# Mamba2 scan with a low-rank mixer on one Trainium2 core: the first batch's transposes split over two banks, the second weight's conversions put elsewhere, and the later loads paced

## The chip, the cores and the metric

The kernel runs on one core of one Trainium2 chip. The metric is the device time in microseconds (us) of one execution; the figure for the kernel before is the median of 7 runs. One execution was also profiled: every instruction of TensorE (PE, with its weight loads as PEld), VectorE (DVE), ScalarE (ACT), GpSimd (POOL) and of SyncE's DMA queue (SP) has a start and a duration there.

## The reference

The first half is a chunked state-space scan over x (4 batches, 8 heads, 768 steps, 32 channels) with B and C (16 states) and a decay a. The second half mixes the tokens through a low rank, then applies a two-layer network to the channels.

```python
# for each batch, head and chunk of the sequence
CB = C_chunk @ B_chunk.T                          # scores
y_intra = (CB * L) @ x_chunk                      # L = exp(cum_i - cum_j), causal
y_inter = (C_chunk @ state) * exp(cum)
state = decay_full * state + sum_j(B_j x_j exp(cum_last - cum_j))
# then, with x = y of all heads, (4, 768, 256)
h = x.T @ U @ V                                   # U 768x32, V 32x768
u = x + h.T
out = u + relu(u @ w_ch1) @ w_ch2                 # w_ch1 256x1024, w_ch2 1024x256
```

x, a, B and C are float32. U, V and the two weights arrive as float64, so the kernel loads their 64-bit words and makes float32 of them itself.

## The kernel before, in words

**Tiling.** A batch's 768 steps are three pairs of 128-step blocks; the twelve pairs of the four batches are numbered k = 0 to 11 (pairs 0 to 2 are batch 0). For a pair, `prep` (L339, DVE) multiplies B and C by decay factors into `BC`. `decayed` (L351, POOL) makes `bd`. `turning` (L363) transposes the four 128x128 pieces of `BC` on PE, and ACT copies them out as `T` (both B and C) and as `Cm` (C, twice, each time masked to one of the two heads of a 32-row group). `gram` (L398) multiplies B by `Cm` into four PSUM banks, and `mask` (L410, DVE) applies causality to give `M`. `state` (L429, PE) and `update` (L444, DVE, then POOL for `Sm`) carry the state on. `inter` (L499) and `intra` (L528) add both parts of y in two `y` banks, and `yout` (L542, ACT) copies them to `yT`. `inter` comes in two parts, and the first product of part 1 is made to wait for some instruction that comes after part 0: the entry `behind["part"]`, which `apart` (L469) sets to a one-column copy that waits for part 0.

**The mixer** of a batch: `ytokening` (L551) transposes `yT` back to `ytok`; `project` (L579) multiplies by U into `pT`; `mixed` (L592) multiplies by V and adds into `yT`. `spread` (L884) puts V on all partition groups first. For batch 0, `up` (L696) then makes `gT` = relu(u @ w1) in 16 steps (m = 0 to 7, two halves each; `some(2)` runs one m), and `whole` (L806) and `down` (L708) multiply by w2. Batches 1 to 3 use a form with fewer products (`quad`, L623; `down`'s p1 to p7), which needs sums of weight blocks (`operands`, L1010) and sums of gT blocks (`sums`, L716).

**Weights.** `to_fp32` (L299) converts one load in three steps: (1) DVE `e` and `top`, ACT `rest`; (2) ACT `power`; (3) three DVE instructions. The loads in order are U with V, two eighths of w1, three quarters of w1, and four quarters of w2. `convert(n)` (L865) issues the next n steps. `convert_ahead` (L869) issues steps 1 and 2 of the next load but one and then step 3 of the current one. Of w2's four quarters, before, steps 3 come at m = 3, m = 5, before m = 6 and before m = 7.

**Order.** The order on every engine is written out by hand: L906 to L996 for batch 0, then the loop at L1028, where iteration k runs pieces of the mixer, the transposes of pair k + 2, `inter(k, 0)`, `gram(k + 1)`, `intra(k)`, `state(k + 1)`, `mask(k + 1)`, `inter(k, 1)`, `yout(k)` and `update(k + 1)`. Iterations 3 and 4 hold the last pieces of batch 0's `up`; iteration 5 begins with the two `whole`. [...]

**Loads.** All loads stand on SP's queue in program order, ahead of all stores of the output (`store`, L757). A pair has six: B and C of each block (64 KB each) and x of each block (128 KB each). Pairs 4 to 11 follow the weights. A pair's buffers are one of six.

**PSUM.** There are eight banks, two under each of the tags w, x, z and y, taken in turn. `gram` uses `xxzz`. `fill(n)` makes the next bank begin with an idle product of n x 128 columns, whose result is overwritten (L82).

```python
        if engine:                                # L386, in turning
            nc.scalar.copy(out=s["T"][:, :, c:c + n], in_=tp)
    turn(0, 1, 1, "w", nc.vector)                 # L913: Cm by DVE, then T by ACT, one bank
    for pieces in plan[:2]:                       # L996: iterations 3 and 4 begin with
        pieces.insert(0, convert_ahead)           # steps of w2's conversion
        if k + 2 < last:                          # L1052
            prep(k + 2)
            decayed(k + 2)
```

Of the kernel before, what the change touches and what calls it, by code (L numbers as in the profile page):

```python
# [9 lines left out]
FP32 = mybir.dt.float32  # L10
# [5 lines left out]
ALU = mybir.AluOpType  # L16
# [4 lines left out]
def kernel(  # L21
# [64 lines left out]
    def bank(tag, *dims):  # L86
        t = psum.tile([P, *dims], FP32, tag=tag, name=tag, bufs=BANKS[tag])
        if fills[0]:
            idle(t if len(dims) == 1 else t.rearrange(
                {2: "p a b -> p (a b)", 3: "p a b c -> p (a b c)"}[len(dims)]), fills[0])  # L90
        fills[0] = 0
        return t

    def fill(n):


        fills[0] = n
# [7 lines left out]
        in_=a.rearrange("(g b) h (c s) -> g (b h c) s", g=2, s=P).rearrange(  # L105
            "g r s -> r g s"))

    x_sb, bc_sb = {}, {}
    pairs = [(b, q) for b in range(NB) for q in range(NPR)]

    def load_bc(k, blocks=(0, 1)):
        b, q = pairs[k]
        if k not in bc_sb:
            bc_sb[k] = raw.tile([P, 2, 2, NH, N], FP32, tag="bc", name="bc")
        for c in blocks:
            for i, src in enumerate((B, C)):
                nc.sync.dma_start(
                    out=bc_sb[k][:, i, c],
                    in_=src[b, :, ts(2 * q + c, P), :].rearrange("h s n -> s h n"))

    def load_x(k, blocks=(0, 1)):
        b, q = pairs[k]
        if k not in x_sb:
            x_sb[k] = raw.tile([P, 2, NH, D], FP32, tag="x", name="x")
        for c in blocks:
            nc.sync.dma_start(
                out=x_sb[k][:, c],
                in_=x[b, :, ts(2 * q + c, P), :].rearrange("h s d -> s h d"))


    UV = const.tile([P, 2, NC * RK], FP32)
# [49 lines left out]
    for m in range(0, NM, 2):  # L181
        load_words(w2[:, m:m + 2],
                   w22[m * P:(m + 2) * P].rearrange("(m p) d -> p m d", p=P))
    for k in range(NPR + 1, NB * NPR):
        load_bc(k)
        load_x(k)


    ident = const.tile([P, P], FP32)
# [170 lines left out]
                :, :, None].to_broadcast([P, n * NH, N]),  # L360
            op=ALU.mult)

    def turning(k, c=0, n=2, tag="w", engine=None):  # L363

        s = st[k]
        if c == 0:
            s["T"] = att.tile([P, 2, 2, P], FP32, tag="T", name="T", bufs=3)
            s["Cm"] = att.tile([P, 2, 2, P], FP32, tag="Cm", name="Cm", bufs=3)
        tp = bank(tag, 2, n, P)
        for i in range(2):  # L370
            for v in range(n):
                if i or v:
                    yield
                nc.tensor.transpose(out=tp[:, i, v],  # L374
                                    in_=s["BC"][:, i, c + v].rearrange("p h n -> p (h n)"),
                                    identity=ident)
        if not engine:
            nc.scalar.copy(out=s["T"][:, :, c:c + n], in_=tp)
        for i in range(2):
            if engine:  # L380
                engine.tensor_scalar(out=s["Cm"][:, i, c:c + n], in0=tp[:, 1],
                                     scalar1=slot[:, i, None], scalar2=None, op0=ALU.mult)
            else:
                nc.scalar.activation(s["Cm"][:, i, c:c + n], tp[:, 1], AF.Copy,  # L384
                                     scale=slot[:, i, None])
        if engine:  # L386
            nc.scalar.copy(out=s["T"][:, :, c:c + n], in_=tp)
# [10 lines left out]
    def gram(k):  # L398
        s = st[k]
        s["g"] = g = four("xxzz", 2, 2, H)  # L400
        for c in range(2):
            for p in range(2):
                for r in range(4):
                    rows, cols = ts(r, Q), ts(p, H)
                    nc.tensor.matmul(  # L405
                        out=g[r][cols, c], lhsT=s["T"][rows, 0, c, cols],
                        rhs=s["Cm"][rows, :, c, cols], start=(c == 0), stop=True,
                        skip_group_check=True)
# [165 lines left out]
    def mixer(b):  # L574
# [4 lines left out]
        def project(c0=0, c1=NC):  # L579

            if c0 == 0:
                hold["p"] = bank("w", P)
            p = hold["p"]
            for c in range(c0, c1):
                for q in range(4):
                    nc.tensor.matmul(out=p[ts(q, Q)], lhsT=U_sb[:, c],  # L586
                                     rhs=ytok[b][:, c, ts(q // 2, P)],
                                     start=(c == 0), stop=(c == NC - 1), skip_group_check=True)
            if c1 == NC:
                nc.scalar.copy(out=pT, in_=p)  # L590

        def mixed():  # L592

# [289 lines left out]

    def spread():  # L884

        v = [bank("y", HS // 2) for _ in range(2)]
        for q in range(4):
            for i in range(2):
                rows = ts(2 * (q % 2) + i, Q)
                nc.tensor.matmul(out=v[i][ts(q, Q)], lhsT=ident[rows, rows], rhs=Vq[rows],  # L890
                                 start=True, stop=True, skip_group_check=True)
        for i in range(2):
            nc.scalar.copy(out=V4[:, ts(i, HS // 2)], in_=v[i])

    def hold(load, until):

        tc.add_manual_dep(load.ins, until.ins.name, mybir.DependencyInfo(
            mybir.DependencyClass.Sync, mybir.DependencyReason.DATA))

    one, others = slice(0, 1), slice(1, NB)  # L900
    yT[0] = mix.tile([P, NCB, S], FP32, tag="yT", name="yT")
# [8 lines left out]
    prep(0, 1, 1)  # L910
    decayed(0)
    fill(1)
    turn(0, 1, 1, "w", nc.vector)  # L913
    fill(2)
    gram(0)
    prep(1, 0, 1)
# [20 lines left out]
    prep(2, 1, 1)  # L937
    decayed(2, 1, 1)
    update(1)
    turn(2, 1, 1, "x", nc.vector)  # L940
    intra(1)
    fill(1)
    gram(2)
    state(2)
    hold(held[0], mask(2, (0, 1)))
    update(2)
    hold(held[2], mask(2, (2, 3)))
    inter(1, 0)
    apart(nc.scalar.copy)
    inter(1, 1)  # L950
    yout(1)
    convert(2)
    fill(1)
    ytokens(0, "x")
    intra(2)
    inter(2, 0)
    apart(nc.vector.tensor_copy)
    inter(2, 1)
    yout(2)
    ytokens(1)  # L960
    convert(1)
    fill(1)
    ytokens(2, "z", (nc.vector.tensor_copy,) * 2)
    spread()
    convert(3)
    next(steps.pop(0))
    project()
    mixed()
    convert(2)
    convert(2)  # L970
# [7 lines left out]
    keep(others)  # L978
    prep(3)
    decayed(3)  # L980
    convert_ahead()
    some(2)
    convert_ahead()
    some(2)
    turn(3)
    prep(4)
    decayed(4)
    some(2)
    gram(3)
    state(3)  # L990
    mask(3)
    update(3)
    convert_ahead()
    some(2)
    turn(4)
    for pieces in plan[:2]:  # L996
        pieces.insert(0, convert_ahead)


    ws = const.tile([P, 5, DF // 2], FP32)  # L1000
# [27 lines left out]
    for k in range(NPR, last + 1):  # L1028
        b, q = divmod(k, NPR)
        pieces = plan[q] if q or b == 1 else []  # L1030
        turns = [turning(k + 2).__next__] * 4 if k + 2 < last else [lambda: None]
        if k > NPR:
            tokens = [ytokening(k - 1).__next__] * 3
            if q == 0:
                late = downs
                project, mixed, ups, plan, downs = mixer(b - 1)
                p4 = late.pop()
                pieces = (late[:1] + tokens + late[1:7] + [project] + late[7:11] + [mixed]
                          + late[11:])
# [12 lines left out]
        if k + 2 < last:  # L1052
            prep(k + 2)
            decayed(k + 2)
        run(pieces + turns)
        inter(k, 0)
        if k + 1 < last:
            gram(k + 1)
        else:
            settle()  # L1060
        intra(k)
        if k + 1 < last:
            state(k + 1)
            mask(k + 1)
        inter(k, 1)
        yout(k)
        if k + 1 < last:
            update(k + 1)
        if q == 1:
            run(plan[3])  # L1070
        if k == NPR + 1:
            operands(4, nc.vector)
    run(downs)

# [29 lines left out]
```

## Time and profile before

| | us |
|---|---|
| median of 7 runs | 239.86 |
| lowest and highest run | 238.24, 243.35 |
| the profiled execution, its own time | 240.84 |
| its span, first to last instruction | 239.0 |

| engine | busy us | share of the span | instructions |
|---|---|---|---|
| PE | 228.4 | 96% | 3166 |
| PEld | 175.6 | 73% | 3166 |
| DVE | 155.1 | 65% | 363 |
| ACT | 95.6 | 40% | 245 |
| POOL | 20.6 | 9% | 40 |

The 16 DMA engines moved 14.60 MB in 81909 packets, of which 76052 were under 512 bytes. The row of granted TensorE clock shows 9 tenths or more in all slices.

A row of the timeline is: start, time taken, engine, line, instruction, what is written from what, shapes, how many alike; then in square brackets how long the engine stood idle just before, and what ended the wait. "issue" means that the engine waited for nothing that the profile shows. Durations of neighbours overlap by about 0.1 us, since the next instruction starts before the last one is recorded as ended. The table of windows gives the busy time of each engine in a stretch, with the number of instructions in brackets.

### The profile page before, as it was taken

The numbers are of one execution on the slowest core, as the hardware profiler recorded it, in microseconds if no ns is written. First come the engines' busy times: TensorE is split into PE (matmuls) and PEld (weight loads), VectorE is DVE, ScalarE is ACT, GpSimd is POOL, SyncE is SP. The second block draws the span as 40 slices with busy tenths as digits, with TensorE's granted clock in tenths as the row PEclk, the third lists the DMA queues.
The fourth block names the chain that finished last, engine by engine and source line by source line (L and its number), as shares of the span: only waits on it lengthen the run. The fifth ranks groups of instructions, "written<-read, shape, count | busy, mean of one in ns | idle before, by whom it ended". The sixth has DMA issues, their size and how long they took to land.

```text
span 239.0 us, 7374 instructions
## 1 busy us (share of the span) xinstructions
PE 228.4 (96%) x3166; PEld 175.6 (73%) x3166; DVE 155.1 (65%) x363; ACT 95.6 (40%) x245; POOL 20.6 (9%) x40
## 2 busy tenths in 40 slices
PE   7998899897899999999999999999999999999995
PEld 5666556555688988565799987565799896659994
DVE  3675799797996667475896671556974372478511
ACT  5354558755514312537624112456312014663110
POOL 4221001120330300002021100010000000000000
PEclk9999999999999999999999999999999999999999
DMA  6984959998988810100001010000001011000111
GB/s 80 115 112 137 274 66 313 157 113 95 115 106 105 130 46 0 44 3 3 3 3 47 5 44 17 31 3 0 3 3 47 8 38 44 0 0 3 44 47 45
DMA packets 81909, 14.60 MB, mean 61 GB/s; under 512 B 76052, under 2 KB 80084, under 8 KB 81876
## 3 DMA queue, kind: packets, MB, share of 16 engines
q1 hardware_dynamic: 81876, 14.13, 32.4%
q8 instruction: 25, 0.41, 0.7%
q14 instruction: 8, 0.07, 0.1%
HBM read 10.98 MB, written 3.15 MB: 59 GB/s over the span
## 4 chain that ended last, share of the span: by engine, by line
PE 83%; DVE 10%; ACT 3%; issue 3%; POOL 0%; DVEq 0%; POOLq 0%; ACTq 0%
PE x L741 17%; PE x L633 14%; PE z L741 13%; PE z L633 10%; PE y L537 4%; PE y L515 3%; PE x L405 3%; PE x L816 3%; PE w L557 2%; PE w L586 2%; PE w L438 2%; PE x L82 2%; PE w L374 1%; DVE rest L323 1%; PE x L737 1%
## 5 line engine op out<-in xcount | busy, mean ns | idle before, releaser
L633 PE MATMUL x<-t,ws 128*128 128x384 f32 x72 | 28.7, 496 | 0.0
L741 PE MATMUL x<-w2s,words 128*128 128x128 f32 x176 | 23.2, 275 | 0.0
L741 PEld LDWEIGHTS x<-w2s,words 128*128 128x128 f32 x176 | 21.6, 193 | 0.0
L621 ACT ACTIVATE gT<-gT 128x384 f32<-128x384 f32 x36 | 19.0, 528 | 2.4 <-DVE gT L642 2.3
L465 POOL TENSOR_TENSOR Sm<-S,slot 128x256 f32<-128x256 f32 (+1 forms) x12 | 8.8, 736 | 122.3 <-DVE S L458 91.8
L633 PEld LDWEIGHTS x<-t,ws 128*128 128x128 f32 x72 | 12.5, 190 | 8.0 <-ACT top L638 1.3
L730 DVE TENSOR_TENSOR words<-gT 128x512 f32<-128x512 f32 (+1 forms) x28 | 16.7, 598 | 0.6 <-ACT gT L621 0.6
L642 DVE TENSOR_TENSOR gT<-z,top 128x384 f32<-128x384 f32 x12 | 6.7, 558 | 15.2 <-PE z L633 13.4
L417 DVE TENSOR_TENSOR M<-x,causal 128x256 int32<-128x256 int32 x24 | 9.1, 420 | 9.6 <-PE z L405 8.3
L638 ACT COPY e<-x 128x384 f32<-128x384 f32 x12 | 5.8, 479 | 23.1 <-PE x L633 23.1
L549 ACT COPY yT<-y 128x256 f32<-128x256 f32 x24 | 7.8, 375 | 17.3 <-PE y L515 17.3
L799 ACT COPY o<-x 128x128 f32<-128x128 f32 x11 | 2.9, 266 | 28.6 <-PE x L741 28.6
L458 DVE SCALAR_TENSOR_TENSOR S<-S,kept,w 128x64 f32<-128x64 f32 x40 | 11.2, 280 | 3.5 <-PE w L438 1.8
L405 PE MATMUL x<-Cm,T 32*64 32x128 f32 x192 | 12.0, 291 | 1.1 <-ACT Cm L384 0.7
L701 PE MATMUL x<-yT,w 128*128 128x384 f32 x32 | 12.0, 496 | 0.7 <-DVE yT L601 0.6
L741 PE MATMUL x<-w,gT 128*128 128x128 f32 x88 | 12.6, 285 | 0.0
L676 DVE TENSOR_SCALAR gT<-x 128x384 f32<-128x384 f32 x12 | 6.7, 557 | 9.1 <-PE x L633 9.1
L741 PEld LDWEIGHTS x<-w,gT 128*128 128x128 f32 x88 | 10.8, 191 | 2.3 <-issue 1.6
L741 PE MATMUL z<-w2s,words 128*128 128x128 f32 x88 | 11.9, 278 | 0.0
L356 POOL TENSOR_TENSOR bd<-bc,FD 128x256 f32<-128x256 f32 (+1 forms) x13 | 9.4, 721 | 29.5 <-ACT FD L282 20.0
L537 PE MATMUL y<-M,x 64*32 64x64 f32 x768 | 10.7, 224 | 1.1 <-issue 1.1
L515 PE MATMUL y<-T,Sm 32*64 32x64 f32 x352 | 11.0, 230 | 0.7 <-ACT settled L471 0.4
(179 smaller groups left out, 507.3 us busy)
## 6 DMA issues: line engine op xcount, KB each, us to landing
words<-in_moe_w_ch_dram SPq DMA_DIRECT2D x7, 512.0 KB, 6.0
x<-in_x_dram SPq DMA_DIRECT2D x24, 128.0 KB, 3.4
out_dram<-o SPq DMA_DIRECT2D x11, 256.0 KB, 2.1
bc<-in_B_dram SPq DMA_DIRECT2D x24, 64.0 KB, 3.6
bc<-in_C_dram SPq DMA_DIRECT2D x24, 64.0 KB, 3.0
words<-in_moe_w_ch_dram SPq DMA_DIRECT2D x2, 256.0 KB, 3.5
words<-in_moe_V_dram SPq DMA_DIRECT2D x1, 192.0 KB
words<-in_moe_U_dram SPq DMA_DIRECT2D x1, 192.0 KB, 4.9
```

The source lines that it names most:

```text
L356: nc.gpsimd.tensor_tensor(out=st[k]["bd"][:, c:c + n].rearrange("p c h n -> p (c h) n"), in0=bc_sb[k][:, 0, c:c + n].rearrange("p c h n -> ...
L405: nc.tensor.matmul(out=g[r][cols, c], lhsT=s["T"][rows, 0, c, cols], rhs=s["Cm"][rows, :, c, cols], start=(c == 0), stop=True, skip_group_ ...
L417: done = nc.vector.tensor_tensor(out=M[:, r].bitcast(INT32).rearrange("p c s i -> p (c s) i"), in0=g[r].bitcast(INT32).rearrange("p c s i ...
L458: done = nc.vector.scalar_tensor_tensor(out=new, in0=st["S", b], scalar=kept[:, b, j, None], in1=add, op0=ALU.mult, op1=ALU.add)
L465: nc.gpsimd.tensor_tensor(out=s["Sm"][:, sl], in0=s["S"][:, sl].rearrange("p i (s d) -> p i s d", s=2), in1=slot[:, None, :, None].to_broa ...
L515: product = nc.tensor.matmul(out=y[p][ts(r % 2, H), r // 2, c], lhsT=own[ts(r, Q)], rhs=s["T"][ts(r, Q), 1, c, ts(p, H)], start=fresh(k, p ...
L537: nc.tensor.matmul(out=y[p][ts(i, Q), n, c], lhsT=x_sb[k][half, c, h], rhs=s["M"][half, h // 2, c, h % 2], start=fresh(k, p, [i]), stop=Tr ...
L621: nc.scalar.activation(g, g, AF.Relu)
L633: nc.tensor.matmul(out=X[name], lhsT=lhsT[:, ts(i, P)], rhs=rhs, start=start, stop=True, skip_group_check=True)
L701: nc.tensor.matmul(out=g, lhsT=w1[:, n, ts(m, P)], rhs=uT[:, n, ts(k, HS)], start=(n == 0), stop=(n == NCB - 1))
L730: nc.vector.tensor_tensor(out=S[v][:, lo:hi], in0=l[:, lo:hi], in1=r[:, lo:hi], op=op)
L741: nc.tensor.matmul(out=X[name], lhsT=lhsT[:, i], rhs=rhs[:, i], start=start and u is None and i == 0, stop=True, skip_group_check=True)
```

## The change

1. The helper `hold` moves up. Each of the six loads of pairs 7 to 11 waits until the load two before it has landed. Loads up to pair 6 are as before.
2. `turn(0, 1, ...)` and `turn(2, 1, ...)` become `split`: C is transposed first and into a bank of its own (y or z), B into another (w or x). ACT copies B's half of `T` alone, DVE makes the two halves of `Cm`, and POOL adds them to give C's half of `T`.
3. In batch 0, `inter(1, 0)` and its `apart` go ahead of `state(2)`. The transposes of `ytokens(1)` go between `inter(2, 0)` and `inter(2, 1)`, and `apart` there is ACT's. The last step for U and V, and `spread`, come sooner. `spread` uses x banks and DVE's copies, the tokens of pair 2 are copied by ACT, `pT` of batch 0 by DVE. One idle product before the tokens of pair 0 goes, and so does the one before those of pair 2; there is now one before `spread` and one before `mixed`.
4. Steps 1 and 2 of w2's first quarter come ahead of m = 3 instead of m = 2, its step 3 after m = 4 instead of ahead of m = 3. Step 3 of the second quarter stays ahead of m = 5. Iteration 3 has only steps 1 and 2 of the third quarter. The third's step 3, with the fourth's steps 1 and 2, stands in iteration 4 after `inter(4, 0)`, the fourth's step 3 at the end of iteration 4, ahead of `operands(4)`.
5. `turn(3)` stays ahead of m = 4, with the conversion after it; `prep(4)` and `decayed(4)` come after m = 4. `gram(3)` uses the banks `xzyy`, `turn(4)` y. `prep(5)` and `decayed(5)` come before m = 5 instead of in iteration 3. Iterations 3 and 4 get an `apart`.

```diff
     def load_x / load_bc: every dma_start is appended to `paced`
     for k in range(NPR + 1, NB * NPR):
+        del paced[:-2]
         load_bc(k)
         load_x(k)
+        if k > NPR + 3:
+            for i in range(2, len(paced)):
+                hold(paced[i], paced[i - 2])
...
+    def split(k, c, tags):
+        s = st[k]
+        tp = {}
+        for i in (1, 0):
+            tp[i] = bank(tags[i], P)
+            nc.tensor.transpose(out=tp[i], in_=s["BC"][:, i, c].rearrange("p h n -> p (h n)"),
+                                identity=ident)
+        nc.scalar.copy(out=s["T"][:, 0, c], in_=tp[0])
+        for i in range(2):
+            nc.vector.tensor_scalar(out=s["Cm"][:, i, c], in0=tp[1], scalar1=slot[:, i, None],
+                                    scalar2=None, op0=ALU.mult)
+        nc.gpsimd.tensor_tensor(out=s["T"][:, 1, c], in0=s["Cm"][:, 0, c], in1=s["Cm"][:, 1, c],
+                                op=ALU.add)
...
-                nc.scalar.copy(out=pT, in_=p)
+                (nc.scalar.copy if b else nc.vector.tensor_copy)(out=pT, in_=p)
...
-    turn(0, 1, 1, "w", nc.vector)
+    split(0, 1, "wy")
...
-    turn(2, 1, 1, "x", nc.vector)
+    split(2, 1, "xz")
     intra(1)
     fill(1)
     gram(2)
+    inter(1, 0)
+    apart(nc.scalar.copy)
     state(2)
     hold(held[0], mask(2, (0, 1)))
     update(2)
     hold(held[2], mask(2, (2, 3)))
-    inter(1, 0)
-    apart(nc.scalar.copy)
     inter(1, 1)
     yout(1)
     convert(2)
-    fill(1)
-    ytokens(0, "x")
+    tokens = [ytokening(0, "x"), ytokening(1)]
+    for _ in range(2):
+        next(tokens[0])
     intra(2)
     inter(2, 0)
-    apart(nc.vector.tensor_copy)
+    apart(nc.scalar.copy)
+    next(tokens[0])
+    convert(1)
+    for _ in range(2):
+        next(tokens[1])
     inter(2, 1)
     yout(2)
-    ytokens(1)
+    next(tokens[1])
     convert(1)
     fill(1)
-    ytokens(2, "z", (nc.vector.tensor_copy,) * 2)
     spread()
-    convert(3)
+    convert(1)
+    ytokens(2, "z")
+    convert(1)
+    project()
     next(steps.pop(0))
-    project()
+    fill(1)
     mixed()
...
-    convert_ahead()
     some(2)
     convert_ahead()
     some(2)
     turn(3)
+    some(2)
+    convert_ahead()
     prep(4)
     decayed(4)
-    some(2)
-    gram(3)
+    gram(3, "xzyy")
     state(3)
     mask(3)
     update(3)
-    convert_ahead()
+    prep(5)
+    decayed(5)
+    convert(1)
     some(2)
-    turn(4)
-    for pieces in plan[:2]:
-        pieces.insert(0, convert_ahead)
+    turn(4, 0, 2, "y")
...
-        if k + 2 < last:
+        if NPR + 2 < k + 2 < last:
             prep(k + 2)
             decayed(k + 2)
         run(pieces + turns)
         inter(k, 0)
+        if k < NPR + 2:
+            apart(nc.scalar.copy)
+            (convert_ahead if k > NPR else lambda: convert(2))()
...
         if k == NPR + 1:
+            convert(1)
             operands(4, nc.vector)
```

More of the change, by code (lines that the diff above doesn't have):

```diff
@@ L106, with hold @@
             "g r s -> r g s"))
-    x_sb, bc_sb = {}, {}
+    x_sb, bc_sb, paced = {}, {}, []
     pairs = [(b, q) for b in range(NB) for q in range(NPR)]
+    def hold(load, until):
+        tc.add_manual_dep(load.ins, until.ins.name, mybir.DependencyInfo(
+            mybir.DependencyClass.Sync, mybir.DependencyReason.DATA))
     def load_bc(k, blocks=(0, 1)):
@@ L116, in load_bc @@
             for i, src in enumerate((B, C)):
-                nc.sync.dma_start(
+                paced.append(nc.sync.dma_start(
                     out=bc_sb[k][:, i, c],
-                    in_=src[b, :, ts(2 * q + c, P), :].rearrange("h s n -> s h n"))
+                    in_=src[b, :, ts(2 * q + c, P), :].rearrange("h s n -> s h n")))
     def load_x(k, blocks=(0, 1)):
@@ L125, in load_x @@
         for c in blocks:
-            nc.sync.dma_start(
+            paced.append(nc.sync.dma_start(
                 out=x_sb[k][:, c],
-                in_=x[b, :, ts(2 * q + c, P), :].rearrange("h s d -> s h d"))
+                in_=x[b, :, ts(2 * q + c, P), :].rearrange("h s d -> s h d")))
     UV = const.tile([P, 2, NC * RK], FP32)
@@ L361, in decayed, with laid, turning @@
             op=ALU.mult)
-    def turning(k, c=0, n=2, tag="w", engine=None):
+    def laid(k):
+        st[k]["T"] = att.tile([P, 2, 2, P], FP32, tag="T", name="T", bufs=3)
+        st[k]["Cm"] = att.tile([P, 2, 2, P], FP32, tag="Cm", name="Cm", bufs=3)
+    def turning(k, c=0, n=2, tag="w"):
         s = st[k]
         if c == 0:
-            s["T"] = att.tile([P, 2, 2, P], FP32, tag="T", name="T", bufs=3)
-            s["Cm"] = att.tile([P, 2, 2, P], FP32, tag="Cm", name="Cm", bufs=3)
+            laid(k)
         tp = bank(tag, 2, n, P)
@@ L376, in turning @@
                                     identity=ident)
-        if not engine:
-            nc.scalar.copy(out=s["T"][:, :, c:c + n], in_=tp)
+        nc.scalar.copy(out=s["T"][:, :, c:c + n], in_=tp)
         for i in range(2):
[L380 to L387, printed above, removed]
-        yield
+            nc.scalar.activation(s["Cm"][:, i, c:c + n], tp[:, 1], AF.Copy,
+                                 scale=slot[:, i, None])
+        yield
+    def split(k, c, tags):
[11 more added lines that the diff above has]
+                                op=ALU.add)
     def turn(*args):
@@ L396, in four, with gram @@
         return [bank(tags[r], *dims) for r in range(4)]
-    def gram(k):
+    def gram(k, tags="xxzz"):
         s = st[k]
-        s["g"] = g = four("xxzz", 2, 2, H)
+        s["g"] = g = four(tags, 2, 2, H)
         for c in range(2):
@@ L884, in spread @@
     def spread():
-        v = [bank("y", HS // 2) for _ in range(2)]
+        v = [bank("x", HS // 2) for _ in range(2)]
         for q in range(4):
@@ L892, in spread @@
         for i in range(2):
[L893 to L898, printed above, removed]
+            nc.vector.tensor_copy(out=V4[:, ts(i, HS // 2)], in_=v[i])
     one, others = slice(0, 1), slice(1, NB)
```

## The prediction

> **What bounds the kernel now.** I read the table of windows first, cut at the first product of `up` (30.3 us), the transposes of pair 5 (54.2) and the first product of `down` (77.06).
>
> ```profile
> core 0: us, PE busy (x) PEld busy (x) DVE busy (x) ACT busy (x) POOL busy (x), PEclk, DMA share, GB/s
> ...
> 14.70:30.30 15.60, 12.99 (x388) 8.92 (x388) 11.31 (x36) 8.23 (x24) 1.72 (x4) 1.00 0.76 189
> 30.30:54.20 23.90, 22.74 (x140) 13.78 (x140) 21.95 (x47) 16.10 (x36) 2.67 (x4) 1.00 0.90 163
> 54.20:77.06 22.86, 20.82 (x529) 16.58 (x529) 18.71 (x39) 9.31 (x22) 3.94 (x4) 1.00 0.85 103
> 77.06:239.00 161.94, 159.00 (x1912) 127.34 (x1906) 95.72 (x214) 55.24 (x146) 7.50 (x10) 1.00 0.09 25
> ```
>
> After 77.06 PE is the bound, and its work doesn't change: whatever comes must come before `down` starts, and moves the end by as much. Before 77.06 PE and DVE are both nearly full, so a wait removed on one counts only up to what the other allows. Then PE's waits, from the timeline:
>
> ```profile
> 23.44 0.30 PE L537 MATMUL y<-M,x 64*32 64x64 f32 x3 [0.47 <-issue]
> ...
> 46.01 0.70 PE L405 MATMUL x<-Cm,T 32*64 32x128 f32 x3 [0.69 <-ACT Cm L384]
> ...
> 54.24 0.63 PE L374 MATMUL w<-ident,BC 128*128 128x128 f32 x4 [0.43 <-DVE BC L344]
> ...
> 58.78 0.42 PE L438 MATMUL w<-x,bd 64*32 64x64 f32 x21 [1.10 <-issue]
> ...
> 65.13 0.53 PE L537 MATMUL y<-M,x 64*32 64x64 f32 x34 [0.63 <-issue]
> ```
>
> Two waits are for ACT and DVE, three for nothing shown. Counting PE's and PEld's instructions, the three come at numbers 961, 1729 and 1985, each 193 above a multiple of 256, and each ends 1.4 to 1.6 us after a packet of 16384 bytes on the instruction queue (landed 21.87, 57.37, 63.74). [...] The packet ahead of the last gap stands in the DMA view of 62.8 to 63.8; the view of 58.8 to 62.8 has none:
>
> ```profile
> q8 instruction: 1, 0.02, 5.5%
> ```
>
> Last, DVE where iterations 3 to 5 hand over to `down`:
>
> ```profile
> 46.24 0.69 DVE L344 TENSOR_TENSOR BC<-bc,F 128x512 f32<-128x512 f32 x1 [0.99 <-DMA bc<-in_C_dram]
> ...
> 59.28 1.31 DVE L458 SCALAR_TENSOR_TENSOR S<-S,kept,w 128x64 f32<-128x64 f32 x4 [1.17 <-PE w L438]
> ...
> 61.11 1.10 DVE L323 SCALAR_TENSOR_TENSOR rest<-top,rest 128x512 f32<-128x512 f32 x1
> ...
> 75.63 0.76 DVE L417 TENSOR_TENSOR M<-x,causal 128x256 int32<-128x256 int32 x2 [1.81 <-PE z L405]
> ```
>
> At 75.63 DVE has only 1.81 us in hand.
>
> **Part by part.**
>
> *First batch.* `split(0, 1)`: DVE no longer waits for the second transpose, ACT no longer for DVE. But the idle product ahead of `gram(0)` runs from 8.37 to 9.43, and `gram(0)` started at 9.36: about 0. `split(2, 1)`, the moved `inter(1, 0)` (wait of 0.37) and the dropped idle product (0.5) bring PE sooner to the end of `intra(2)`. There stands the block edge of 23.44 (an idle product less moves it by 4 instructions). The packet started at 20.86, 1.5 us after PE entered the block before (19.34), and that entry was itself 1.5 us behind a packet. So these savings turn into a longer gap; I allow 0.2. After the edge: inter part 1 waits for DVE's copy 0.34 less; against that the chain ACT `yT`, transposes, `ytok`, `project`, `pT`, `mixed` stays, and on ACT `ytok` of pair 2 now queues behind `rest` and `power` of the first eighth of w1 (0.47 and 0.51). `pT` queues on DVE behind that eighth's three instructions (0.42 each): U and V's conversion starts without the wait for `settled` (24.38 before, 23.5 now), so they end near 28.2 and `mixed` starts near 28.4 against 28.75. I take 0.4 for all of this; ends -0.3 (the queues on ACT and DVE come late) and 1.7 (the waits of 0.37, 0.34, 0.47, 0.46 all go). DVE gains two copies of V (ACT took 0.55 for both) and `pT` (0.27 on ACT) and loses two of tokens (0.76): even. POOL's two sums are nearest to L356's products of 128x128, 0.4 each. None of the moved steps issues a DMA. `mask(2)`'s second half, which frees the last three loads of w1, comes some 0.3 later behind `state(2)`; the first of these landed at 28.01 and was used at 32.69, so that is covered. Beside DVE POOL's sums can stretch one DVE instruction by 0.4, and DVE has waits of 0.96 and 1.25 behind them.
>
> *Iterations' approach.* ACT's `rest` and `power` of w2 no longer stand ahead of T and Cm of pair 3, and these have m = 4 (2.9 us) to be ready: 0.69 gone. With `xzyy`, `gram(3)` no longer waits piecewise for the relu of m = 4: it took 1.36 us (46.01 to 47.37), the unhindered one at 63.33 took 0.76: 0.6 gone. `prep(5)` ahead of m = 5 removes 0.43; it waits for pair 5's C (landed 50.55), with the second quarter's step 3, M(4) and all later DVE work queued behind; BC is needed at about 52.6, so 1.4 us cover it. `turn(4)` in y needs M(3), free 1 us before. So PE reaches `inter(3, 0)` 0.4 + 0.69 + 0.6 + 0.43 = 2.1 us sooner. Then `gram(4)` loses its waits for relus (1.68 us with them: 0.9 gone), but runs into the edge at 1729. The `apart` of iterations 3 and 4 costs ACT 0.19 each and waits for `inter(k, 0)`; behind it stand only conversion steps and `yout`, which PE feeds 2 us later, and ACT has 13.5 us idle in this window.
>
> [...] 58.78 - 2.1 = 56.7. I take 56.7; ends 55.7 (`inter(3, 0)` through at 52.9, an estimated 0.5 to the start as the unloaded packets have it, 0.9 for the packet, 1.4) and 58.78 (packet no sooner, as DMA is full to the same time).
>
> *Pacing.* SP's loads of pair 7 began at 53.97 and are the traffic under the next packet, which started 4.1 us after the edge at 58.78; unloaded, later ones start within 1.4 in most cases. With two loads in flight I take the 0.63 as gone (ends 0 and 0.63). Waiting loads hold up SP's queue: pairs 7 to 11, then the stores. Six loads by twos at 3.3 us take 9.9 us a pair: pair 7's B and C are there by 63 (`prep` at 70.1), pair 8's by 73 (78.1), pair 9's by 83 (107.5), the last x by 106. The first store moves from 81 to 106; the three output buffers cover that until the fourth group, whose store came at 127. Cost 0.
>
> *w2's conversions.* From S(4) to M(6) DVE worked 59.28 to 75.63 less 0.18, 0.59 and 1.81. Now one conversion more falls into it: 0.67 (e, top, start to start) and 2.02 (three instructions at 54.68, without POOL) or 2.9 (at 61.11, beside POOL). S(4) starts 0.5 after the resumption, so M(6) can start 0.5 + 13.8 + 2.7 = 17.0 us after it (17.8 beside POOL): 73.7 to 74.5. PE would be there at 75.63 - 2.1 - 0.63 = 72.9, with up to 0.5 more if w2's last quarter (ready at 66.0 to 66.8) is late for its product in `whole(0)` (66.3). So DVE decides: 75.63 - 73.9 = 1.7 us, ends 1.1 and 1.9. PE's gain of 2.7 is partly handed to DVE.
>
> **Sum.** The profiled execution goes from 240.84 (span 239.0 and 1.84 around it) to 239.1. It lay 0.98 above the median; from 239.86 the 1.7 us give 238.2.
>
> **Rivals.**
> - *Pacing frees the packets, 0.30.* Resumption at 55.7, M(6) at 72.7 to 73.5, and the first batch gives 0.5 more: about 3 us, 236.9. For: DMA share 0.85 to 0.90 there. Against: pair 6's loads are unpaced and on the wires until 56.9. With all first-batch waits gone it reaches 235.6.
> - *As forecast, 0.39:* 237.6 to 238.8.
> - *Gains eaten, 0.19.* The packet for 1729 comes at 57.5 to 58.5, M(6) at 74.5 to 75.5: 239.3. It includes that pacing does nothing for packets: at 72.64 one started without delay at full DMA load.
> - *DVE becomes late, 0.12, slower.* The packet comes as before (58.78) and both conversions of iteration 4 run beside POOL at 1.10 an instruction: M(6) at 58.78 + 17.0 + 1.7 = 77.5, 1.9 us late, 241.8. It decides as soon as resumption is later than 56.9 at these durations, later than 58.6 at the uncontended ones.
>
> **Chances.** A measurement of this kernel tells about 0.5% (1.2 us) from no change. Faster by more: 0.30 and most of 0.39, 0.66; within: 0.22; slower: 0.12. The range, 235.6 to 240.4, reaches into the third case's far side and leaves out the slow one.
>
> **What would show it.** Right: no wait at `gram(3)` nor at the transposes of pair 5; a gap of "issue" in `state(4)` ending 1.4 us after a packet, near 56.7; none in `intra(4)`; DVE without idle time ahead of M(6) near 73.9; `down` from about 75.4. Wrong: `mixed` before 27.5 (the early edges were no bound), `state(4)` without a gap, DVE still idle by over 1 us ahead of M(6) (PE decides), or SP's held loads late for pair 7 or 8.

## The result, and the profile after

The kernel after the change takes 236.82 us (median of 14 runs, 235.6 to 240.38). The ratio to the kernel before is 0.9894, with a 95% interval of 0.9872 to 0.9916: 2.5 us gained (2.0 to 3.1), where 1.7 were forecast. The medians of all runs differ by 3.0; the ratio leaves out the slower executions of either kernel, most of which had a lower granted clock. The profiled execution went from 240.84 to 237.23 us, its span from 239.0 to 235.5. In the profile all of this lies ahead of `down`, whose first product came at 73.23 instead of 77.06.

The table of windows of the kernel after, cut at the first product of `up` (29.06), near the end of pair 5's transposes (51.75) and at the first product of `down` (73.20):

```profile
core 0: us, PE busy (x) PEld busy (x) DVE busy (x) ACT busy (x) POOL busy (x), PEclk, DMA share, GB/s
...
14.70:29.06 14.36, 12.94 (x389) 8.64 (x389) 11.41 (x36) 8.34 (x23) 1.94 (x4) 1.00 0.80 203
29.06:51.75 22.69, 22.69 (x171) 14.25 (x176) 19.80 (x43) 15.60 (x35) 2.44 (x4) 1.00 0.92 168
51.75:73.20 21.45, 19.40 (x515) 15.40 (x498) 20.00 (x43) 10.27 (x25) 3.67 (x4) 1.00 0.60 73
73.20:235.50 162.30, 159.35 (x1914) 127.52 (x1906) 95.66 (x215) 55.27 (x146) 7.50 (x10) 1.00 0.14 31
```

From `up` to the end of the transposes PE now has no idle time at all. The stretch behind it still leaves PE 2 us idle and DVE 1.4; the DMA share there is 0.60, with the loads of pairs 7 to 11 held. The last stretch is as long as before to 0.4 us.

The timeline of PE in the kernel after, with the transposes of pair 5 and all waits over 0.3 us between `mixed` and `down` but one (0.63 ahead of `up`, as long before), and the one gap in the first batch:

```profile
22.39 0.21 PE L558 MATMUL y<-M,x 64*32 64x64 f32 x1 [0.42 <-issue]
...
50.82 0.63 PE L387 MATMUL w<-ident,BC 128*128 128x128 f32 x4
...
54.61 0.41 PE L459 MATMUL w<-x,bd 64*32 64x64 f32 x20 [1.33 <-issue]
...
60.70 0.48 PE L558 MATMUL y<-M,x 64*32 64x64 f32 x33 [0.37 <-issue]
...
65.21 1.13 PE L837 MATMUL x<-w,gT 128*128 128x256 f32 x4 [0.35 <-DVE w L336]
```

The waits for `Cm` at `gram(3)` and for `BC` at pair 5's transposes are gone. `gram(3)` itself took 0.70 us (44.00 to 44.70) instead of 1.44 (46.01 to 47.45, first start to last end). Three gaps of "issue" remain: 0.42, 1.33 and 0.37 (before: 0.47, 1.10 and 0.63). But the one in `state(4)` ends 4.17 us sooner than before, where 2.1 were forecast. The wait at 65.21 is new: the first `whole` waits for w2's last quarter, which DVE (L336) has just made.

The timeline of DVE in the kernel after:

```profile
45.61 0.69 DVE L353 TENSOR_TENSOR BC<-bc,F 128x512 f32<-128x512 f32 x1 [1.60 <-DMA bc<-in_C_dram]
...
49.68 0.99 DVE L353 TENSOR_TENSOR BC<-bc,F 128x512 f32<-128x512 f32 x1 [0.89 <-DMA bc<-in_C_dram]
...
55.11 1.31 DVE L479 SCALAR_TENSOR_TENSOR S<-S,kept,w 128x64 f32<-128x64 f32 x4 [0.51 <-PE w L459]
...
71.80 0.76 DVE L438 TENSOR_TENSOR M<-x,causal 128x256 int32<-128x256 int32 x2 [0.51 <-PE z L426]
```

DVE runs from 55.11 to 71.29 without a pause and is then idle for 0.51 ahead of M(6), instead of 1.81. `prep(4)` and `prep(5)` wait for their loads of C, 1.60 and 0.89 us.

### The profile page after: what moved, and what is told of

Same layout as the page of the kernel before. It is cut to its first block, busy times and chain, and to the rows that moved or that the text cites. A ratio compares the mean times of both kernels' runs of the same rounds, so it can differ in the third digit from the quotient of the medians.

```text
span 235.5 us, 7378 instructions
## 1 busy us (share of the span) xinstructions
PE 227.2 (96%) x3166; PEld 174.9 (74%) x3166; DVE 154.3 (66%) x363; ACT 96.1 (41%) x246; POOL 21.1 (9%) x42
## 4 chain that ended last, share of the span: by engine, by line
PE 91%; DVE 6%; issue 1%; POOL 0%; ACT 0%; DVEq 0%; POOLq 0%
PE x L762 17%; PE x L654 14%; PE z L762 13%; PE z L654 10%; PE x L722 4%; PE y L558 4%; PE z L722 4%; PE y L536 3%; PE w L607 3%; PE x L426 2%; PE x L82 2%; PE x L837 2%; PE w L459 2%; PE w L578 2%; PE w L387 1%; PE x L758 1%
## 5 line engine op out<-in xcount | busy, mean ns | idle before, releaser
L353 DVE TENSOR_TENSOR BC<-bc,F 128x512 f32<-128x512 f32 (+1 forms) x15 | 9.4, 628 | 4.3 <-DMA bc<-in_C_dram 2.5
L762 PE MATMUL z<-w,gT 128*128 128x128 f32 x88 | 11.6, 275 | 0.0
L722 PE MATMUL z<-yT,w 128*128 128x384 f32 x32 | 11.6, 486 | 0.0
```

The lines of the kernel that those rows point to most:

```text
L353: nc.vector.tensor_tensor(out=st[k]["BC"][:, :, c:c + n].rearrange("p i c h n -> p i (c h) n"), in0=bc_sb[k][:, :, c:c + n].rearrange("p i ...
L722: nc.tensor.matmul(out=g, lhsT=w1[:, n, ts(m, P)], rhs=uT[:, n, ts(k, HS)], start=(n == 0), stop=(n == NCB - 1))
L762: nc.tensor.matmul(out=X[name], lhsT=lhsT[:, i], rhs=rhs[:, i], start=start and u is None and i == 0, stop=True, skip_group_check=True)
```

## The experiments

Two theories stood against each other. **A:** the gaps of "issue" fall at fixed counts of PE's instructions, and the packets ahead of them come at places of PE's own program whatever the traffic; the gain is the waits removed from `up` and `gram(3)`, plus the packet in `state(4)`, which comes sooner with PE; from S(4) on, DVE sets the time. **B:** the packets are late because of the loads, and the pacing frees them. Beside them stands the question of what the first batch gives. The expectations also name theories C and D, which differ from run to run and are told in each expectation.

The numbers of instructions here and in the prediction count the records of PE and PEld in the trace, PE's semaphore waits included (6332 and 49 in the kernel before). The three gaps of "issue" come at 961, 1729 and 1985, so 768 and 256 apart; without the waits they stand at 951, 1711 and 1965, which are not multiples of 256 apart. In the same span the instruction queue moved 25 packets of 16384 bytes, one for 255 records. "Block" is only a name here for 256 records, counted up and down from 961, and "edge" for where one ends. Of the 25 edges in the profile before, those three show a gap of "issue" over 0.3 us on PE. What PE lacked there is not shown: the trace has the gaps and, 1.57, 1.41 and 1.39 us ahead of their ends, a packet's landing (21.87, 57.37 and 63.74). Each ratio is against the kernel before, on the same chip.

The table is worked out from the profiles: distances in us between first products (`inter` is `inter(3, 0)`, `whole` the first one). A version's first batch, middle (parts 4 and 5 of the change) and pacing are those of before (b) or after (a).

| version | batch, middle, pacing | `up` to `inter` | `inter` to `whole` | `whole` to `down` | ratio, 95% interval |
|---|---|---|---|---|---|
| before | b b b | 24.49 | 11.75 | 10.51 | 1 |
| e2_pace | b b a | 24.49 | 10.93 | 10.51 | 0.9994 (0.9958 to 1.003) |
| e3_first | a b b | 24.49 | 9.59 | 10.54 | 1.0018 (0.999 to 1.0046) |
| e4_middle | b a b | 22.26 | 9.51 | 11.34 | 0.9926 (0.9901 to 0.9951) |
| e1_nopace | a a b | 22.64 | 10.87 | 11.59 | 0.992 (0.9895 to 0.9946) |
| after | a a a | 22.32 | 10.72 | 11.13 | 0.9894 (0.9872 to 0.9916) |
| after_again | a a a | 22.93 | 10.99 | 11.19 | 0.9897 (0.9847 to 0.9947) |

### The parts alone

**e1_nopace**, the kernel after without the waits of the loads:

```diff
-        if k > NPR + 3:
+        if k > NB * NPR:
             for i in range(2, len(paced)):
```

> The changed kernel without the waits of the loads of pairs 7 to 11; all else as changed. Theory A [...]: the packet ahead of the gap in intra(4) still starts while PE is at the transposes of pair 6, near 58.5 us, the gap there stays at 0.3 to 0.5 us, and the time is that of the changed kernel within 0.3 us. Theory B (the traffic of the loads delays the packets): the packet starts 0.5 to 1 us later, the gap grows to 0.9 or more, and the kernel is 0.6 to 1.5 us slower than the changed one.

Measured: 237.67 us, 0.992. The timeline of PE in this version:

```profile
55.26 0.41 PE L459 MATMUL w<-x,bd 64*32 64x64 f32 x20 [1.20 <-issue]
...
61.62 0.48 PE L558 MATMUL y<-M,x 64*32 64x64 f32 x33 [0.64 <-issue]
```

The gap in `state(4)` is no longer than with pacing (1.33). The one in `intra(4)` is 0.64, against 0.37 in the first profile of the kernel after, but see its second profile below.

**e2_pace**, the kernel before with the waits of the loads alone (the first hunk of the diff).

> The kernel before with the paced loads alone. Theory A: the gap of 0.63 us in intra(4) and that of 1.10 us in state(4) stay within 0.2 us, time 239.9 within 0.5 us. Theory B: the gap in intra(4) goes, 0.6 us faster. Both: the held loads land in time, nothing waits for them.

Measured: 239.48 us, 0.9994. First a row of the table of windows of the kernel before, 60 to 64 us, its last two columns the DMA share and GB/s; then the same of e2_pace; then PE's gaps in e2_pace:

```profile
60.00:64.00 4.00, 4.00 (x64) 2.71 (x62) 3.90 (x6) 2.40 (x7) 2.02 (x2) 1.00 1.09 129
```

```profile
60.00:64.00 4.00, 3.64 (x91) 2.52 (x89) 3.79 (x7) 2.75 (x6) 1.83 (x2) 1.00 0.45 58
```

```profile
57.92 0.42 PE L447 MATMUL w<-x,bd 64*32 64x64 f32 x21 [0.28 <-issue]
...
64.27 0.54 PE L546 MATMUL y<-M,x 64*32 64x64 f32 x34 [0.63 <-issue]
```

The traffic ahead of the packet fell by more than half, and the gap in `intra(4)` stayed at 0.63. The packet started 99 instructions of PE and PEld behind the edge at 1729, as in the kernel before (99 too; 93 in the kernel after). That is A's reading, and B falls for this gap. For the gap in `state(4)` A's expectation failed: it was to stay within 0.2 of 1.10, but the packet came 0.44 sooner here and the gap was 0.28. That pacing shortens it isn't shown either, since the kernel after has 1.33 with pacing and 1.20 without.

**e3_first**, the first batch's part alone, with the middle and the loads of before.

> The kernel before with the first batch's part alone (both split transposes, the moved inter, tokens, spread, conversions and copies), loads not paced. Theory A (block edges move with PE's progress): the block edge at the end of intra(2) comes near 22.4 us instead of 23.44, mixed starts near 27.5, up near 29.1, and the whole is about 1.2 us faster, less what the edge in state(4) and DVE keep: 0.8 to 1.3. Theory C (the edges are a clock of their own, as the prediction had it): mixed no sooner than 28.3, 0.4 us faster.

Measured: 240.49 us, 1.0018. The interval leaves a gain of 0.24 us at most, so both expectations (0.8 to 1.3 and 0.4) failed. In its profile `mixed` came at 29.68, later than before. But there PE met a gap of 1.68 at an earlier edge (number 705), and the granted clock from 14.7 to 29 us was 0.88 (1.00 before), so this position doesn't tell the part's worth. The timeline of PE:

```profile
20.73 0.27 PE L426 MATMUL x<-Cm,T 32*64 32x128 f32 x1 [1.68 <-issue]
```

Its second distance is 2.2 us shorter than before's: the packet for `state(4)` landed at 52.98, ahead of `inter(3, 0)` (55.72), and both gaps are gone. This profile loses 0.9 of that ahead of `up` and 1.0 behind `down`; no gain of that size is in the times. What one profile shows of the gaps need not hold in every execution.

**e4_middle**, the middle alone, with the first batch and the loads of before.

> The kernel before with the middle part alone (w2's conversions, turn and prep moved, the banks of gram(3) and turn(4), apart in iterations 3 and 4), loads not paced. Theory A: inter(3, 0) 2.2 us sooner than before (52.6), down's first product 2.3 to 2.7 us sooner, 2.0 to 2.5 us faster in all. Theory C: the edge in state(4) keeps 1 us of it and DVE is late with M(6), 1.0 to 1.5 us faster.

Measured: 237.81 us, 0.9926. This part alone brings 1.8 us (1.2 to 2.4), most of the whole change. That lies between what A (2.0 to 2.5) and C (1.0 to 1.5) expected, and decides neither. Its profile has 3.6 us from `up` to `down`, but it is of an execution as fast as the fastest of the 20 (236.68, median 237.81), with a gap of only 0.17 in `state(4)`.

**after_again**, the kernel after unaltered, for the scatter.

> The changed kernel unaltered, once more, for its scatter. All theories: 0.9894 of before within its interval. Theory D (the packets' waiting time scatters from execution to execution by half a microsecond to a microsecond, so one profile doesn't settle the first batch): mixed anywhere between 27.3 and 29.3 us though the program up to there is the same in four kernels now. Theory A (place in the program sets it): mixed within 0.3 us of 27.5.

Measured: 237.88 us, 0.9897. Its profile has the gap in `intra(4)` at 0.64, so the 0.37 of the first profile is scatter, and not the pacing. `mixed` came at 28.00, against 27.50 in the first: more than the 0.3 that A allowed, as D expected.

### The block edges

**e5_early128** and **e6_late128** move every later edge by 128 instructions (half a block), with small products whose results are overwritten: e5 ahead of pair 2's transposes in place of an idle product, e6 ahead of the first product of `up`. The 32 products of e6 are 64 records of PE in its trace (11 and 53, below). e5 sets two expectations against each other: one in case the distance of the edges is the bound between 14 and 24 us (4.10 us from 705 to 961 before, 19.34 to 23.44), one in case the chain of work is.

```diff
+            nc.tensor.matmul(out=t[rows, :Q], lhsT=ident[rows, rows], rhs=ident[rows, rows], ...)
...
+    tiny(bank("y", P), 32)                       # e6
     some(2)
```

> The changed kernel with 132 more such instructions in place of the idle product ahead of the transposes of pair 2 (15.4 us), where PE waits until 16.3 us anyway. [...] mixed 1.2 to 2.2 us later, although the products themselves fit in the wait, and 1 to 2 us slower in all. If the chain of work bounds there: mixed within 0.3 us (against theory D within its scatter), no change in time.

> The changed kernel with 128 more PE instructions (32 products of 32 x 32 into an unused bank, matmuls and loads of weights in two passes each) ahead of up's first product, where PE stood idle for 0.63 us; they change no result. Every later block edge comes 128 instructions sooner in the program. Theory A/D [...]: no gap in state(4) and none in intra(4); instead one gap of 0.8 to 1.5 us at the edge in state(5) or intra(4)'s end of the iteration before whole; time within 0.6 us of the changed kernel. Rival (the gaps belong to the place in the work, or to DMA traffic at that time): gaps stay in state(4) and intra(4) at 54 to 55 and 60 to 61 us.

Measured: e5 238.69 us, 0.997 (0.9931 to 1.0009); e6 238.33 us, 0.9914 (0.9881 to 0.9947). e5's `mixed` came at 30.33, 2.3 to 2.8 us later than in the kernel after (1.2 to 2.2 were expected), but its granted clock was 0.76 between 14.7 and 29 us, so that the small products aren't shown to be the cause. Its time, 1.8 us above the kernel after, is in the expected range, but in 7 of its 14 executions the mean granted clock was 0.979 to 0.993, against 2 of 15 of the kernel after: inconclusive. In e6 the timeline of PE has the edge elsewhere:

```profile
29.03 0.31 PE L90 MATMUL y<-ident 32*32 32x32 f32 x11
30.55 0.66 PE L90 MATMUL y<-ident 32*32 32x32 f32 x53 [1.22 <-issue]
31.14 0.59 PE L729 MATMUL x<-yT,w 128*128 128x384 f32 x1
```

The edge numbered 1217, which in the kernel after falls among `up`'s long products and shows no gap, now falls among the small products and costs 1.22. The gaps in `state(4)` and `intra(4)` are gone, as expected: `inter` to `whole` took 9.08 us. So in e6 the gaps did not stay at their place in the work. The gap of 0.8 to 1.5 that was expected at a later edge was 0.17; the one among the small products was not expected. What was won behind was paid ahead.

**e12_split** moves the edges without added work, by cutting `up`'s products for m = 1 to 4 in three.

```diff
+            parts = 3 if b == 0 and 1 <= m <= 4 else 1
+            for c in range(parts):
+                cols = ts(c, HS // parts)
                 for n in range(NCB):
-                    nc.tensor.matmul(out=g, ..., rhs=uT[:, n, ts(k, HS)],
+                    nc.tensor.matmul(out=g[:, cols], ..., rhs=uT[:, n, ts(k, HS)][:, cols],
```

> The version after with the products of up for m = 1 to 4 cut in three pieces of 128 columns: the same columns and sums, but 64 more products and as many weight loads, so every block edge behind up stands 128 instructions earlier in the program. From the product row, 0.348 us for 384 columns and about 0.115 for 128, the pieces themselves should cost nothing (at most 0.1 us each for four steps if the weight loads show). Theory C (the gaps of 1.33 in state(4) and 0.37 to 0.64 in intra(4) come from where the edges fall, and what they cost is the 1.4 us by which S(4) comes later; from there DVE decides): no issue gap in state(4) or intra(4), first update of iteration 3 some 2.3 us after inter(3,0) instead of 3.7, w2's last quarter still waited for by 0.4 to 0.9 in the first whole, down 1.2 to 1.6 us sooner counted from up; ratio near 0.984. Theory D (the gaps are slack that DVE would take anyway, as it stays busy from S(4) on): gaps gone but down at the same distance from up, ratio 0.990 as before.

Measured: 237.66 us, 0.9891 (0.985 to 0.9933). The timeline of PE:

```profile
53.72 0.54 PE L459 MATMUL w<-x,bd 64*32 64x64 f32 x30
...
59.08 0.86 PE L558 MATMUL y<-M,x 64*32 64x64 f32 x64
...
60.70 0.44 PE L536 MATMUL y<-T,Sm 32*64 32x64 f32 x11 [0.21 <-issue]
...
64.33 0.92 PE L841 MATMUL x<-w,gT 128*128 128x256 f32 x3 [0.23 <-DVE w L336]
```

`state(4)` and `intra(4)` run through, and `up` to `inter` took 22.66, so the cut cost nothing that can be seen. From `up` to `down` it is 42.78 us, 1.4 to 2.3 less than in the two profiles of the kernel after; theory C expected 1.2 to 1.6. The time is rather against C: 0.9891, where C's 0.984 lies just outside the interval and D's 0.990 inside. The profiled execution was one of the faster ones (236.28 us, median 237.66).

### Who decides behind S(4)

**e10_ahead** puts steps 1 and 2 of w2's third quarter ahead of `prep(5)` instead of in iteration 3.

> The changed kernel with steps 1 and 2 of w2's third quarter put ahead of prep(5), where DVE stood idle for 0.89 us waiting for pair 5's loads, instead of in iteration 3. If DVE decides (the prediction's step): the wait of whole(0) for w2 (0.35 us) goes and down starts 0.4 to 0.7 us sooner. If PE decides: at most the 0.35 us, and 0 if DVE's work merely moves behind the prep that turn(5) needs.

Measured: 238.09 us, 0.992 (0.9889 to 0.9951). The first `whole` still waited 0.35 for w2's last quarter. What was moved had stood ahead of S(4), and the chain behind it was untouched: the edit missed the work that it meant to relieve. And `gram(4)` waited for relus again (1.80 us in all, against 0.85), since ACT's moved steps now stand ahead of them.

**e11_lastq** changes only the order within the two `whole`:

```diff
+                whole(0, 0, NM - 2)
+                begun(1)
+                whole(1, 0, 4)
+                whole(0, NM - 2, NM)
+                whole(1, 4, NM)
```

> The version after with only the order of the products in the two whole changed: the first whole's products with w2's last quarter come behind the second whole's first half, so PE has 1.1 us or more of other work while DVE finishes that quarter. In all five profiles of the version after and its variants M(6) came 6.6 us after these products began, and they began when DVE was done, with 0.35 to 0.55 us of waiting. Theory 'DVE decides, through w2's last quarter': wait gone, M(6) 0.36 sooner, DVE's idle time ahead of it 0.51 down to about 0.15; 0.3 us of time, ratio near 0.9885. Theory 'PE decides through its own edges': no change in down's distance from the resumption of state(4), ratio 0.990.

Measured: 237.6 us, 0.9898 (0.9861 to 0.9936). The timelines of PE, then of DVE:

```profile
65.21 2.76 PE L839 MATMUL x<-w,gT 128*128 128x256 f32 x12
67.80 0.38 PE L831 MATMUL x<-ident,yT 128*128 128x128 f32 x2
```

```profile
74.31 0.75 DVE L438 TENSOR_TENSOR M<-x,causal 128x256 int32<-128x256 int32 x2
```

Neither PE in `whole` nor DVE ahead of M(6) waits any more. M(6) came 16.86 us after `state(4)` resumed (57.45), against 17.19 in the kernel after and 17.47 in its second profile: 0.3 to 0.6 less, where "DVE decides" expected 0.36. The time can't resolve this.

**e13_both** is e11 with e12. (The "first quarter" in its expectation is the first half, as in e11.)

> The cut of up's products together with the order of e11 (the two products groups of whole that use w2's last quarter put behind the second whole's first quarter). Theory C with DVE deciding by w2's last quarter: both gains add, 1.4 for the edges and 0.4 to 0.9 for the wait that is left: ratio near 0.982, PE without a wait in either whole, and DVE's idle time ahead of M(6) near zero. If PE alone decides after S(4): as e12, 0.984. If neither counts: 0.990.

Measured: 237.38 us, 0.9888 (0.9856 to 0.9921). No wait in `whole`, none ahead of M(6), and `whole` to `down` is back at 10.51. But its profile has a gap of 1.31 in `inter(4, 1)`, behind a packet that landed at 60.13, at the edge where e12, with the same program of PE up to there, had 0.21. The timeline of PE:

```profile
61.57 0.44 PE L536 MATMUL y<-T,Sm 32*64 32x64 f32 x11 [1.31 <-issue]
```

The expected 0.982 lies below the interval. No version is shown to beat the kernel after.

**e7_xxzz** gives `gram(3)` its old banks:

```diff
-    gram(3, "xzyy")
+    gram(3)
...
-    turn(4, 0, 2, "y")
+    turn(4)
```

> The version after with gram(3) in the banks xxzz again and pair 4's transposes in w. If the banks xzyy are what took the piecewise waits for ACT's relu out of gram(3) (a step of 0.6 us in the prediction), gram(3) waits again and inter(3,0) comes some 0.6 us later counted from up, 0.2 to 0.6 us of time: ratio 0.991 to 0.992. If what hindered gram(3) was Cm alone, which now comes early in both, nothing changes: 0.990.

Measured: 239.03 us, 0.9943 (0.99 to 0.9985), some 1.2 us above the kernel after, with intervals that just overlap. The timelines of PE and DVE:

```profile
45.66 0.32 PE L426 MATMUL z<-Cm,T 32*64 32x128 f32 x1 [0.21 <-ACT gT L727]
...
48.84 1.56 PE L722 MATMUL x<-yT,w 128*128 128x384 f32 x4 [2.07 <-DVE M L438]
```

```profile
47.76 0.69 DVE L353 TENSOR_TENSOR BC<-bc,F 128x512 f32<-128x512 f32 x1 [1.31 <-DMA bc<-in_C_dram]
48.37 0.75 DVE L438 TENSOR_TENSOR M<-x,causal 128x256 int32<-128x256 int32 x2
```

`gram(3)` took 1.32 us again, waiting for a relu, as expected. More came on top: m = 5 needs a bank that M(3) still reads, and M(3) stands on DVE behind `prep(4)`, which waits 1.31 for the load of C. So `inter(3, 0)` came 25.00 us behind `up`, 2.1 to 2.7 later than in the kernel after, not 0.6. About half of it came back: the gap in `state(4)` was gone, since its packet started 0.90 ahead of `inter(3, 0)` (54.17), instead of 0.44 behind it.

## Why the prediction was right, and where it was not

**All gain ahead of `down`: right.** From `down` to the end took 161.95 us before and 162.30 after; over the other versions 161.98 to 162.96.

**First batch, 0.4: not resolved.** `mixed` came 1.25 us sooner in the two profiles shown, at 27.50, on the mark below which "the early edges were no bound" was to follow. But that is mostly scatter: the three profiles with before's first batch have it at 28.75, 28.70 and 28.12, seven with the new one (clock undiminished) at 27.46 to 28.51. The difference of the means is 0.6. In the times e3 leaves at most 0.24. The edge of the end of `intra(2)` still costs 0.42 in the profile after (0.47 before), as forecast, but nothing in the second profile.

**`up` to `inter(3, 0)`, 0.69 + 0.6 + 0.43 = 1.7: right.** Measured 2.17, and 1.6 to 2.2 over the versions with the whole middle. The term of 0.6 for the banks is exact in itself (1.32 in e7 against 0.70), but the working missed what else the banks do: with `prep(4)` and its late load on DVE ahead of M(3), the old banks cost a further wait of 2.07 in e7.

**Resumption of `state(4)` at 56.7 (ends 55.7 and 58.78): wrong, and the term that was mis-sized.** It came at 54.61, sooner than the early end. That a gap stays was right (1.33), and so was that it ends 1.4 behind the packet (landed 53.20). But "58.78 - 2.1" took the gain of `gram(4)` as swallowed whole, and the packet as tied to `inter(3, 0)` with its old delay; that was the author's estimate, from the one profile before. Measured: `inter(3, 0)` came 3.42 sooner, of which 1.25 is the first batch of this profile; the packet started 0.44 behind it instead of 1.14; it took 1.38 instead of 1.43. The sum, 3.42 + 0.70 + 0.05, is the 4.17.

**Pacing removes the 0.63 in `intra(4)`: wrong.** It stayed 0.63 with the pacing alone, at less than half of the traffic, and was 0.64 in the second profile of the kernel after. The reading behind the step doesn't hold either: of the 14 edges behind 84 us in the profile before, where no loads are left, only 7 have the next packet within 1.4 us; for the others it came 3.4 to 19.0 us later. What the pacing gives in time is not resolved: 0.9894 and 0.9897 with it, 0.992 without, intervals overlapping. The rival "pacing frees the packets" came nearest in number (236.9) with a mechanism that the runs don't bear out.

**DVE needs 17.0 to 17.8 us from the resumption to M(6), and decides: right in the profiles.** It was 17.19 (17.47 twice in the other profiles). The form differs a little: DVE holds PE at w2's last quarter (0.35 at 65.21, forecast as up to 0.5), and M(6) then follows PE by 6.6 us; e11 took that detour out, and DVE had no idle time left. With the resumption at 54.61 in place of 56.7 the forecast's own sum gives M(6) at 71.6 to 72.4; it came at 71.80.

**Held loads, cost 0: right.** Pair 7's C landed at 60.76 for a `prep` at 67.61. The first store was issued at 92.50 instead of 81.16, and nothing waited for it.

**The time: range right, size too small.** The 1.7 forecast, and its ends of 1.1 and 1.9 for the last step, lie below the 2.0 to 3.1 measured; of the sum's terms the resumption was put too late. The range held because it took in the other cases. The forecast had 0.4 and 1.7 up to `inter(3, 0)` and then 0.4 lost, as DVE takes over: 1.7. The profile has 1.25 and 2.17, then 0.41 gained up to `down` (1.03 ahead of the first `whole`, 0.62 lost in it and behind) and 0.35 lost behind: 3.48 of the span. The times, in which the scatter of the first batch averages out, give 2.5. Why e3 and e12 show 1.4 to 2.3 us in the profile and not in the time, and e4 3.6 against 1.8, stays open. One reason is near: executions of one program of PE have other gaps. e2_pace has before's program of PE and 0.28 in place of 1.10, e13 has e12's up to `whole` and 1.31 in place of 0.21. How often each occurs wasn't measured.

## What to carry to other kernels

For gaps that end at nothing shown ("issue"), count the records of PE and PEld, semaphore waits included: here the three stood 768 and 256 apart, and with 128 instructions more ahead of the last two these were gone (e6, e12). A gain upstream of such a gap is not lost whole: in `state(4)` 4.17 us came through where 2.1 were forecast. When a step that waits for a load is moved up, look at what stands behind it on its engine and which bank that frees: in e7 M(3) stood on DVE behind `prep(4)`, which waited 1.31 us for its load, and PE waited 2.07 for M(3). Here, in the profiles, the bank choice was worth more (2.1 to 2.7 us) than the wait it was meant for (0.6). One profile's positions carry about 1 us of chance at this size, so a part's worth is read from distances that repeat (24.49 in three profiles) and from the times.

## What the runs showed of the hardware beyond what was expected

With 128 instructions more, with more work (e6) or without (e12), the gaps of 1.33 in `state(4)` and 0.37 in `intra(4)` were gone; e6 had 1.22 ahead of `up` instead, e12 0.21 in `inter(4, 1)`. The packet ahead of the gap in `intra(4)` starts at nearly the same place in PE's program (86 to 99 instructions behind the edge before it in nine profiles with unmoved edges, 99 before and 93 after; 70 in e3), but that for `state(4)` does not (6 to 103 in those nine, 52 before and 84 after). Behind 99 us, where no loads are left, 13 of 14 packets start at the same places in the profiles before and after, to 8 instructions; but these places lie 1 to 253 instructions behind an edge in the profile before. What sets them is open. Gaps of "issue" over 0.3 us ended 1.2 to 1.6 us after a packet had landed (1.57, 1.41 and 1.39 before; 1.40, 1.41 and 1.30 after).

The granted clock was not at 1.00 in every profile. This is the row of granted clock, in 40 slices, of the kernel after and of e11:

```profile
PEclk9999999999999999999999999999999999999999
```

```profile
PEclk9995899999999999999999999999999999999999
```

Four of the fourteen profiles have such a dip. Their mean granted clock over the span was 0.993 (e3) and 0.986 (e5, e10, e11), against 0.999 to 1.000 in the other ten; if the dip was to half of full speed (the 5 in e11's row), that is an estimated 3.3 us in e3 and 6.6 to 6.7 in the others. From 14.7 to 29 us it was 0.88 in e3 and 0.76 in e5 and e10; in e11 the low slices are those from 17.9 to 29.8. In the four `mixed` came at 29.68 to 30.52 instead of 27.46 to 28.75. In e3 PE had been idle for 1.68 us ahead of 20.73, and in e10 it was busy for 11.55 of the first 14.70 us, against 12.84 in the kernel after, so in these two part of the delay is idle time. The gap of 1.33 in `state(4)` and the wait of 2.07 in e7 are in profiles with a mean clock of 1.000: that such a wait brings a dip isn't shown. Positions of such profiles are compared above only from `up` on.
